# Moving the choice of batches 2 and 3 and their MLP two to three steps earlier in a fused retention and mixture-of-depths kernel

## The chip, the cores and the metric

The kernel runs on one core of one Trainium2 chip. The metric is the device time of one execution in microseconds (us). Engines are named as in the profile: PE is TensorE's matrix unit, PEld its weight load, DVE is VectorE, ACT is ScalarE, POOL is GpSimd, SP is SyncE, which here only starts transfers.

## The reference: what is computed

Eight batches, eight heads, 576 positions, head size 64. First a retention layer (attention without softmax, with a causal decay per head), then a mixture of depths: in each batch the 128 positions with the highest score get a two-layer MLP added, all others pass unchanged.

```python
scores = scale * np.matmul(q, k.transpose(0, 1, 3, 2))
ret = scores * Dmat                 # gamma_h ** (i - j) for j <= i, else 0
x = np.matmul(ret, v)               # bridged to (batch, position, 512)
s = np.einsum('bsd,d->bs', x, w_gate)
top_idx = np.argpartition(-s[b], 128)[:128]
ye = np.maximum(x[b, top_idx] @ w1, 0.0) @ w2          # 512 -> 1024 -> 512
out[b, top_idx] = x[b, top_idx] + sigmoid(s[b, top_idx])[:, None] * ye
```

## The kernel before

**Steps.** The program is one unrolled loop (line 660 on) over 36 steps and one more that drains; 9 steps make a group of two batches (`NC = 9`, `NG = 4`). Steps 0 to 8 are the "wide" group: a step is 128 positions, batches 0 and 1 one after the other. Steps 9 to 35 are three "pair" groups: a step is 64 positions of two batches side by side, so batches 2 and 3 are steps 9 to 17, batches 4 and 5 steps 18 to 26, batches 6 and 7 steps 27 to 35. The decays are carried as a running state `u_ps`, copied out to `st`, so that each step needs only its own block of scores and the state of the step before.

**A pair step on PE.** PE executes in the order in which the program is written. Step s issues, interleaved two by two: the scores `sc_ps` of step s with the value products `y_ps<-vs,am` of step s-1 (call this A); then a piece of MLP work; then the state sums `u_ps` of step s with the state products `y_ps<-st,raw` of step s-1 (call this B). DVE masks the scores (`am`, line 340), scales the result (`xs`, line 356) and forms the gate score of each position (`scored`, line 365). ACT scales the values (`vs`, line 224, eight instructions of one head each) in pair steps; in wide steps POOL does it in one instruction (line 219). POOL starts the stores of `xs`.

**Loads.** SP loads 256 KB pieces, four a step. From step 15 on a piece is started at a moment of PE's program (`tick`, line 153): one at the start of A, one behind A, one behind the MLP piece, one at the start of B. In the stretch that the change touches, step s starts the pieces of step s+2, and the last two of them are those that A needs.

**Choice.** When a group's nine steps are scored, PE spreads the scores along a row (`n_spread`, or `w_spread` for the wide group), ACT copies the row, DVE counts for each position how many are higher (`n_compare`, `n_late`, line 458: 576 columns wide for three of the nine blocks, 192 for six), turns ranks into one-hot rows (`n_chosen`, `hot`, nine instructions), PE turns these into indices (`n_fetch`, `idx_ps`), ACT casts them, and POOL gathers the 128 chosen rows of each batch from HBM (line 423, one indirect DMA a batch).

**MLP.** `mlp` and `ups` transpose the gathered rows on PE (`xg_ps`, line 504, in program order, at once) and put the rest into a queue of parts. `some(n)` takes n parts of the queue. A part of the upward product (`h_ps`) or of the downward one (`ye_ps`) has a size by how many batches it serves: for batches 0 and 1 each on its own (called half parts here, 4 matmuls of `ye_ps` or 16 narrow ones of `h_ps` in the profile), for batches 2 and 3 together (whole parts, 8 of `ye_ps` or 16 of `h_ps`), for batches 4 and 5 upward in half parts again (8 of `h_ps`). When a batch's last downward part is through, DVE forms `o` (line 530), which frees the one PSUM bank that `ye_ps` has, and POOL scatters the rows.

**The order.** A table written by hand, `at(step, place, function, ...)`, sets at which place of a step each function is issued; places 1, 2, 2.5 and 3 stand behind A, behind the MLP part, behind the wide results, and at the step's end. `n_parts` says how many parts each step takes between places 1 and 2.

**What the change and the prediction touch:** `scaled` (line 215), the table entries for the wide group's second spread (lines 597 to 599), for group 1's choice, gather and MLP (lines 623 to 632), `n_parts` (line 647), and the loop's calls of `scaled` (lines 669 and 692).

Of the kernel before, what the change touches and what calls it, by code (L numbers as in the profile page):

```python
# [13 lines left out]
OP = mybir.AluOpType  # L14
# [5 lines left out]
P = 128  # L20
# [27 lines left out]
def kernel(  # L48
# [17 lines left out]
    NS = qkvk.shape[0]  # L66
    DM, F = 512, 1024
    KD, FB = DM // P, F // P
    D = DM // H
    NG = len(KINDS)  # L70
    NC = NS // NG
# [3 lines left out]
    MIX = NC // 2  # L75
# [98 lines left out]
    decw = part_of("decw", 2 * NC * H).rearrange("p (s c h) -> p s c h", s=2, c=NC)  # L174
    dec = part_of("dec", 2 * NC * H).rearrange("p (s c h) -> p s c h", s=2, c=NC)
# [19 lines left out]
    def tables():  # L195
        nc.vector.tensor_scalar(aheadw[:, BEFOREW : BEFOREW + P], causw, TINY, -TINY,
                                op0=OP.mult, op1=OP.add)
        nc.vector.tensor_scalar(ahead[:, BEFORE : BEFORE + C], caus, TINY, -TINY,
                                op0=OP.mult, op1=OP.add)
        nc.vector.tensor_copy(out=place, in_=part_of("place", 2 * NC).rearrange(  # L200
            "p (a b) -> p a b", b=2))
        nc.vector.tensor_copy(out=placew, in_=part_of("placew", 2 * NC).rearrange(
            "p (a b) -> p a b", a=2))
# [9 lines left out]
    kind = lambda s: KINDS[s // NC]  # L213

    def scaled(s):
        k = s % NC
        vs[s] = work.tile([P, DM], F32, name="vs", bufs=4)
        if kind(s) == "wide":
            return nc.gpsimd.tensor_tensor(out=heads(vs[s]), in0=heads(raw[s][:, 2, :]),
                                           in1=decw[:, 0, k, :].unsqueeze(2).to_broadcast([P, H, D]),  # L220
                                           op=OP.mult)
        else:
            for h in range(H):
                nc.scalar.activation(out=vs[s][:, hd[h]], in_=raw[s][:, 2, hd[h]], func=AF.Copy,  # L224
                                     scale=dec[:, 0, k, h : h + 1])

    wide_heads = [(j, i, HJ * i + j) for j in range(HJ) for i in range(2)]
    jd = [slice(D * j, D * j + D) for j in range(HJ)]
# [2 lines left out]
    def w_scores(s):  # L231
        for i in range(2):
            sc_ps[s, i] = bank("sc_ps", "sc")
        first = None
        for j, i, h in wide_heads:
            ins = mm(sc_ps[s, i][:, jt[j]], raw[s][halves[i], 1, jt[j]],
                     raw[s][halves[i], 0, jt[j]], True, True)
            first = first or ins
        return first

    def w_sums(s):
        k = s % NC
        if k == NC - 1:
            return
        if k in (0, MIX):
            u_ps[s // NC, k >= MIX] = bank("u_ps", "u", 1)
        u = u_ps[s // NC, k >= MIX]
        rows = halves[1] if k == MIX else slice(0, P)
        for j, i, h in wide_heads:
            mm(u[halves[i], jd[j]], raw[s][rows, 3, hd[h]], vs[s][rows, hd[h]],  # L250
               k in (0, MIX) and j == 0, k in (MIX - 1, NC - 2))

    def w_masked(s):
        am[s] = work.tile([P, 2, 512], F32, name="am")
        mask = mixw if s % NC == MIX else causw
        v = lambda t: t.rearrange("p (j t) -> p j t", t=P)
        for i in range(2):
            nc.vector.tensor_tensor(out=v(am[s][:, i, :]), in0=v(sc_ps[s, i]),  # L258
                                    in1=mask.unsqueeze(1).to_broadcast([P, HJ, P]), op=OP.mult)

    def w_state(s):
        if s % NC < NC - 1:
            st[s] = work.tile([P, DM], F32, name="st")
            nc.scalar.copy(out=st[s][:, : HJ * D], in_=u_ps[s // NC, s % NC >= MIX][:, : HJ * D])
# [27 lines left out]
    def n_open(s):  # L292
        k = s % NC
        sc_ps[s] = bank("sc_ps", "sc")
        for h in range(H):
            for half in halves:
                yield lambda h=h, half=half: mm(sc_ps[s][half, hd[h]], raw[s][half, 1, hd[h]],
                                                raw[s][half, 0, hd[h]], True, True)
# [13 lines left out]
    def n_values(s):  # L312
        k = s % NC
        y_ps[s] = bank("y_ps", "y")
        for h in range(H):
            for i, half in enumerate(halves):
                yield lambda h=h, i=i, half=half: mm(
                    y_ps[s][halves[1 - i], hd[h]], am[s][half, 0, hd[h]], vs[s][half, hd[h]],
                    h == 0, k == 0)
# [10 lines left out]
    def in_turn(a, b, moments):  # L330
        for n in range(H):
            for f in (next(a, None), next(a, None), next(b, None), next(b, None)):
                if f:
                    f()
            if n in moments:
                tick(AHEAD if n == 0 else 2)

    def n_masked(s):
        am[s] = work.tile([P, 2, 512], F32, name="am")
        nc.vector.tensor_tensor(out=heads(am[s][:, 0, :]), in0=heads(sc_ps[s]),  # L340
                                in1=caus.unsqueeze(1).to_broadcast([P, H, C]), op=OP.mult)
# [26 lines left out]
    def stored(s):  # L368
        g, k = divmod(s, NC)
        if kind(s) == "pair":  # L370
            nc.gpsimd.dma_start(out=outs[2 * g][k], in_=xs[s])  # L371
        elif k == MIX:
            nc.gpsimd.dma_start(out=outs[2 * g][P * k :], in_=xs[s][:C])
            nc.gpsimd.dma_start(out=outs[2 * g + 1][:C], in_=xs[s][C:])
        else:
            t0 = P * k - (S if k > MIX else 0)
            nc.gpsimd.dma_start(out=outs[2 * g + (k > MIX)][t0 : t0 + P], in_=xs[s])
# [63 lines left out]
    EARLY = 2 * NC // 3  # L441
# [117 lines left out]
    def some(n):  # L559
        for _ in range(min(n, len(parts))):  # L560
            f, a = parts.popleft()
            f(*a)
# [4 lines left out]
    plan = {}  # L567

    def at(slot, where, f, *a):
        plan.setdefault((slot, where), []).append((f, a))  # L570

    def do(slot, where):
        for f, a in plan.get((slot, where), []):
            f(*a)
# [6 lines left out]
    T1, T3, T4, T5 = P * 3, S, P * (MIX + 3), 2 * S  # L581
# [12 lines left out]
    at(7, 2.5, w_fetch, 0, 0)  # L594
    at(9, 3, ups, 0)

    at(7, 2.5, w_spread, 0, MIX, MIX + 3)
    for c in range(MIX, MIX + 3):
        at(8, 1, w_compare, 0, 1, c, T3, T4, 0)
    at(9, 3, w_spread, 0, MIX + 3, NC)  # L600
    for c in range(MIX, MIX + 3):
        at(10, 1, w_compare, 0, 1, c, T4, T5, 1)
# [14 lines left out]
    for g in range(1, NG):  # L617
        s = NC * g + EARLY + 1
# [3 lines left out]
               n_compare, g, c, 0, EARLY)  # L622
    s = 2 * NC
    at(s + 1, 2, n_spread, 1, EARLY, NC)
    for c in range(EARLY, NC):
        at(s + 1, 3, n_late, 1, c)
    for c in range(EARLY):
        at(s + 2, (1, 3)[c // 3], n_late, 1, c)
    at(s + 3, 3, n_chosen, 1)
    at(s + 5, 1, n_fetch, 1)  # L630
    at(s + 7, 1, mlp, 2, 3)
    at(s + 7, 3, gates, 2, 3)
    s = 3 * NC
    at(s + 1, 2, n_spread, 2, EARLY, NC)
    for c in (*range(EARLY, NC), *range(EARLY)):
# [8 lines left out]
    at(s + 4, 3, gates, 4, 5)  # L644


    n_parts = {s: 1 if s < 34 else 2 for s in range(10, 37)}

    def ahead_of(s):
        if s <= LED:  # L650
            load(s, 1)
            load(s, 0)
        if s == 10:
            weight(0)
            weight(1)
# [6 lines left out]
    for s in range(NS + 1):  # L662
        pe["slot"] = s
        ahead_of(s + AHEAD)
        wide = s < NS and kind(s) == "wide"
        before = s > 0 and kind(s - 1) == "pair"
        if wide:
            first = w_scores(s)
            if kind(s + 1) == "wide":
                tc.add_manual_dep(scaled(s + 1).ins, first.ins.name, LANDED, reason="beside scores")  # L670
        if s in range(1, NC + 1) and s != NC - 1:
            stored(s - 1)
        if wide:
            w_sums(s)
            w_masked(s)
            w_state(s)
        else:
            in_turn(n_open(s) if s < NS else iter(()), n_values(s - 1) if before else iter(()),
                    (0,))
            if s < NS:  # L680
                n_masked(s)
        if s == MIX:
            tables()
        tick()
        do(s, 1)
        if s == NC - 1:
            stored(s - 1)
        scattered()
        some(n_parts.get(s, 0))
        tick()  # L690
        do(s, 2)
        if s + 1 < NS and kind(s + 1) == "pair":
            scaled(s + 1)
        if wide:
            w_results(s)
            do(s, 2.5)
            values(s)
        else:
            in_turn(n_sums(s) if s < NS else iter(()), n_states(s - 1) if before else iter(()),
                    (0, H // 2))  # L700
            if s < NS:
                n_state(s)
            if before:
                values(s - 1)
                for x in due.get(s, []):
                    scored(x)
                stored(s - 1)
        do(s, 3)
# [104 lines left out]
```

## Time and profile before

| what | value |
|---|---|
| three runs | 254.56, 255.22, 258.52 us; median 255.22 us |
| the profiled execution's own time | 253.84 us |
| its span in the profile | 252.1 us |
| PE busy | 230.0 us (91%) in 4595 matmuls |
| PEld, DVE, ACT, POOL busy | 177.0, 129.1, 104.8, 47.2 us |
| moved by DMA | 56.97 MB, of it 44.76 MB read from HBM and 11.53 MB written |

The page has a busy strip of 40 slices (6.3 us each) for each engine, the clock granted to PE, the chain of work that ended last, and groups of instructions. Views of the trace add the instructions in order of time ("timeline": start, duration, engine, line, operation, tiles, count, and in brackets the idle time before it and what ended it), the sums of busy time in chosen windows (busy us and instruction count for PE, PEld, DVE, ACT and POOL, then granted clock, DMA share, GB/s), the list of waits (total, times, longest), and the chain in order of time (start, duration, what).

### The profile page before, as it was taken

The numbers are of one execution on the slowest core, as the hardware profiler recorded it, in microseconds if no ns is written. First come the engines' busy times: TensorE is split into PE (matmuls) and PEld (weight loads), VectorE is DVE, ScalarE is ACT, GpSimd is POOL, SyncE is SP. The second block draws the span as 40 slices with busy tenths as digits, with TensorE's granted clock in tenths as the row PEclk, the third lists the DMA queues.
The fourth block names the chain that finished last, engine by engine and source line by source line (L and its number), as shares of the span: only waits on it lengthen the run. The fifth ranks groups of instructions, "written<-read, shape, count | busy, mean of one in ns | idle before, by whom it ended". The sixth has DMA issues, their size and how long they took to land.

```text
span 252.1 us, 10488 instructions
## 1 busy us (share of the span) xinstructions
PE 230.0 (91%) x4595; PEld 177.0 (70%) x4595; DVE 129.1 (51%) x342; ACT 104.8 (42%) x380; POOL 47.2 (19%) x67
## 2 busy tenths in 40 slices
PE   8997998894999979999779999999999998899991
PEld 6796886884998966656448888666688854588440
DVE  3455787582056539995435699536536492300011
ACT  2364365944455853854443455537251200211000
POOL 0624453002010100034002010403120004100011
PEclk9999999999599999999999999999999999999998
DMA  7989999999589869989957776788631102100011
GB/s 239 384 324 400 359 393 373 376 390 401 190 255 303 289 204 328 309 272 326 338 179 248 229 232 235 220 277 267 229 126 45 49 0 75 64 31 0 0 42 42
DMA packets 23085, 56.97 MB, mean 226 GB/s; under 512 B 2944, under 2 KB 3072, under 8 KB 23040
## 3 DMA queue, kind: packets, MB, share of 16 engines
q1 hardware_dynamic: 18864, 42.67, 49.5%
q0 software_dynamic: 4176, 13.63, 14.3%
q8 instruction: 36, 0.59, 1.0%
q14 instruction: 9, 0.07, 0.1%
HBM read 44.76 MB, written 11.53 MB: 223 GB/s over the span
## 4 chain that ended last, share of the span: by engine, by line
PE 72%; DMA 13%; issue 8%; ACT 3%; DVE 2%; POOLq 0%; SPq 0%; DVEq 0%; ACTq 0%
PE h_ps L157 24%; PE ye_ps L157 16%; DMA raw<-in_qkvk 11%; PE y_ps L157 11%; PE u_ps L157 8%; PE sc_ps L157 8%; ACT xs L353 1%; PE row_ps L157 1%; PE xg_ps L504 1%; DMA out<-o,idx 1%; DVE am L258 1%; ACT vs L224 1%; ACT xg L506 1%; DVE o L530 1%; PE idx_ps L157 1%
## 5 line engine op out<-in xcount | busy, mean ns | idle before, releaser
L157 PE MATMUL h_ps<-xg,w_sb 128*128 128x256 f32 (+1 forms) x320 | 62.6, 351 | 3.3 <-issue 1.9
L157 PE MATMUL ye_ps<-w_sb,hT 128*128 128x512 f32 x128 | 58.6, 602 | 0.6 <-DVE o L530 0.6
L157 PEld LDWEIGHTS h_ps<-xg,w_sb 128*128 128x128 f32 x320 | 52.3, 197 | 9.5 <-issue 2.1
L224 ACT ACTIVATE vs<-raw,table 128x64 f32<-128x64 f32 x216 | 54.3, 341 | 0.0
L157 PE MATMUL y_ps<-vs,am 64*64 64x64 f32 (+1 forms) x1152 | 41.9, 222 | 4.1 <-issue 3.5
L356 DVE TENSOR_TENSOR xs<-y_ps,table 128x512 f32<-128x512 f32 x27 | 18.6, 690 | 48.5 <-PE y_ps L157 48.4
L157 PE MATMUL sc_ps<-raw 64*64 64x64 f32 (+1 forms) x1008 | 42.1, 231 | 1.4 <-DMA raw<-in_qkvk 1.4
L157 PEld LDWEIGHTS y_ps<-vs,am 64*64 64x64 f32 (+1 forms) x1152 | 37.3, 136 | 5.3 <-issue 4.1
L157 PEld LDWEIGHTS ye_ps<-w_sb,hT 128*128 128x128 f32 x128 | 23.3, 190 | 24.9 <-issue 23.4
L157 PE MATMUL y_ps<-st,raw 64*64 64x64 f32 (+1 forms) x896 | 39.6, 232 | 1.1 <-ACT xs L353 0.7
L157 PEld LDWEIGHTS u_ps<-vs,raw 64*64 64x64 f32 (+1 forms) x896 | 30.1, 138 | 14.2 <-issue 9.1
L157 PEld LDWEIGHTS sc_ps<-raw 64*64 64x64 f32 (+1 forms) x1008 | 37.5, 145 | 3.3 <-issue 1.3
L371 POOL DMA_DIRECT2D out<-xs x27 | 14.9, 552 | 124.3 <-DVE xs L356 124.3
L157 PE MATMUL u_ps<-vs,raw 64*64 64x64 f32 (+1 forms) x896 | 35.3, 226 | 2.8 <-issue 2.4
L157 PEld LDWEIGHTS y_ps<-st,raw 64*64 64x64 f32 (+1 forms) x896 | 34.1, 144 | 3.5 <-issue 1.6
L518 ACT ACTIVATE hT<-h_ps 128x256 f32<-128x256 f32 (+1 forms) x24 | 10.9, 454 | 56.4 <-PE h_ps L157 56.4
L530 DVE SCALAR_TENSOR_TENSOR o<-ye_ps,gate,xr 128x512 f32<-128x512 f32 x8 | 6.0, 750 | 43.9 <-PE ye_ps L157 23.4
L458 DVE SCALAR_TENSOR_TENSOR scr<-row,sc,ahead 128x384 f32<-128x384 f32 (+2 forms) x45 | 26.0, 578 | 2.7 <-ACT row L451 1.5
L365 DVE SCALAR_TENSOR_TENSOR scr<-xs,wg 128x512 f32<-128x512 f32 x36 | 25.6, 712 | 1.0
L346 ACT COPY st<-u_ps 128x512 f32<-128x512 f32 x24 | 13.8, 575 | 17.0 <-PE y_ps L157 17.0
L340 DVE TENSOR_TENSOR am<-sc_ps,table 128x512 f32<-128x512 f32 x27 | 18.6, 687 | 3.7 <-PE sc_ps L157 1.9
L258 DVE TENSOR_TENSOR am<-sc_ps,table 128x512 f32<-128x512 f32 x18 | 11.6, 686 | 16.8 <-PE sc_ps L157 16.7
(51 smaller groups left out, 129.5 us busy)
## 6 DMA issues: line engine op xcount, KB each, us to landing
raw<-in_qkvk SPq DMA_DIRECT2D x84, 256.0 KB, 4.5
raw<-in_qkvk SPq DMA_DIRECT2D x30, 512.0 KB, 6.2
out<-xs POOLq DMA_DIRECT2D x35, 256.0 KB, 5.1
w_sb<-in_w SPq DMA_DIRECT2D x12, 256.0 KB, 4.2
w_sb<-in_w SPq DMA_DIRECT2D x2, 512.0 KB, 6.5
table<-in_consts SPq DMA_DIRECT2D x1, 314.0 KB, 6.0
wg<-in_w_gate SPq DMA_DIRECT2D x1, 256.0 KB, 4.7
out<-xs POOLq DMA_DIRECT2D x2, 128.0 KB, 6.2
```

Source lines behind the costliest of these rows:

```text
L157: pe["last"] = nc.tensor.matmul(out, w, x, start=start, stop=stop, skip_group_check=True)
L224: nc.scalar.activation(out=vs[s][:, hd[h]], in_=raw[s][:, 2, hd[h]], func=AF.Copy, scale=dec[:, 0, k, h : h + 1])
L258: nc.vector.tensor_tensor(out=v(am[s][:, i, :]), in0=v(sc_ps[s, i]), in1=mask.unsqueeze(1).to_broadcast([P, HJ, P]), op=OP.mult)
L340: nc.vector.tensor_tensor(out=heads(am[s][:, 0, :]), in0=heads(sc_ps[s]), in1=caus.unsqueeze(1).to_broadcast([P, H, C]), op=OP.mult)
L346: nc.scalar.copy(out=st[s], in_=u_ps[s // NC])
L353: nc.scalar.activation(out=xs[s][:, hd[h]], in_=y_ps[s, h // HJ][:, jd[h % HJ]], func=AF.Copy, scale=decw[:, 1, k, h : h + 1])
L356: nc.vector.tensor_tensor(out=heads(xs[s]), in0=heads(y_ps[s]), in1=dec[:, 1, k, :].unsqueeze(2).to_broadcast([P, H, D]), op=OP.mult)
L365: nc.vector.scalar_tensor_tensor(scr, xs[s], 1.0, wg, op0=OP.mult, op1=OP.mult, accum_out=sc[g][:, k : k + 1])
L371: nc.gpsimd.dma_start(out=outs[2 * g][k], in_=xs[s])
L458: nc.vector.scalar_tensor_tensor(scr[:, : C * (c1 - c0)], row[g][:, C * c0 : C * c1], sc[g][:, c : c + 1], ahead[:, at + C * c0 : at + C * ...
L518: nc.scalar.activation(out=hT[group][:, f0 : f0 + n, :w], in_=t, func=AF.Relu)
L530: nc.vector.scalar_tensor_tensor(o[:cap], ye[b][:cap], gate[b][:cap], xr[b][:cap], op0=OP.mult, op1=OP.add)
```

## The change: what it does

- **Values of step 9.** `scaled(9)` is one POOL instruction with the pair decays, in place of eight on ACT. It is issued in step 8 behind the first score matmul.
- **A spread in step 8.** The wide group's second spread (columns 4 to 6, three PE transposes and one ACT copy) moves from step 7, place 2.5, to step 8, place 2; its three compares move from place 1 to place 3 of step 8.
- **Choice of batches 2 and 3.** Six compares at the end of step 19 (three before), the last three in step 20 at place 1, the one-hot rows at the end of step 20 (21 before), indices and gathers in step 21 (23 before).
- **MLP of batches 2 and 3.** The transposes stand at the end of step 22 (before: in step 25), so the eight whole parts run in steps 23 to 30 (before: 26 to 33).
- **Parts.** Steps 19, 20 and 21 take a second half part at their end, so that the queue of batches 0 and 1 is empty after step 22 (before: after step 25). Step 31 takes none; steps 32 to 36 take one half part each of batches 4 and 5 (before: steps 34 to 36 two each). Eleven parts are left for the tail, ten before.

```diff
     def scaled(s):
         k = s % NC
+        by = (decw if kind(s) == "wide" else dec)[:, 0, k, :]
         vs[s] = work.tile([P, DM], F32, name="vs", bufs=4)
-        if kind(s) == "wide":
+        if s <= NC:
             return nc.gpsimd.tensor_tensor(out=heads(vs[s]), in0=heads(raw[s][:, 2, :]),
-                                           in1=decw[:, 0, k, :].unsqueeze(2).to_broadcast([P, H, D]),
-                                           op=OP.mult)
+                                           in1=by.unsqueeze(2).to_broadcast([P, H, D]), op=OP.mult)
...
-    at(7, 2.5, w_spread, 0, MIX, MIX + 3)
+    at(8, 2, w_spread, 0, MIX, MIX + 3)
     for c in range(MIX, MIX + 3):
-        at(8, 1, w_compare, 0, 1, c, T3, T4, 0)
+        at(8, 3, w_compare, 0, 1, c, T3, T4, 0)
...
     s = 2 * NC
     at(s + 1, 2, n_spread, 1, EARLY, NC)
-    for c in range(EARLY, NC):
-        at(s + 1, 3, n_late, 1, c)
-    for c in range(EARLY):
-        at(s + 2, (1, 3)[c // 3], n_late, 1, c)
-    at(s + 3, 3, n_chosen, 1)
-    at(s + 5, 1, n_fetch, 1)
-    at(s + 7, 1, mlp, 2, 3)
-    at(s + 7, 3, gates, 2, 3)
+    for c in (*range(EARLY, NC), *range(EARLY)):
+        at(s + 1 + (c in (3, 4, 5)), 1 if c in (3, 4, 5) else 3, n_late, 1, c)
+    at(s + 2, 3, n_chosen, 1)
+    at(s + 3, 2, n_fetch, 1)
+    at(s + 4, 3, mlp, 2, 3)
+    at(s + 5, 3, gates, 2, 3)
...
-    n_parts = {s: 1 if s < 34 else 2 for s in range(10, 37)}
+    n_parts = {s: int(s != 31) for s in range(10, 37)}
+    for s in (19, 20, 21):
+        plan.setdefault((s, 3), []).insert(0, (some, (1,)))
...
-            if kind(s + 1) == "wide":
+            if s + 1 <= NC:
                 tc.add_manual_dep(scaled(s + 1).ins, first.ins.name, LANDED, reason="beside scores")
...
-        if s + 1 < NS and kind(s + 1) == "pair":
+        if NC < s + 1 < NS:
             scaled(s + 1)
```

**ACT in steps 7 and 8.** Here `idx` is the cast of batch 0's indices, the first `xs` are the eight results of step 7, `row` is the copy of the spread, `vs` the values of step 9 and the next `xs` the results of step 8:

```order
 L264 COPY st<-u_ps 128x256
 L438 CAST idx<-idx_ps 128x1
+L353 ACTIVATE xs<-y_ps,table 128x64 x8
 L390 COPY row<-row_ps 128x384
-L353 ACTIVATE xs<-y_ps,table 128x64 x8
-L224 ACTIVATE vs<-raw,table 128x64 x8
 L353 ACTIVATE xs<-y_ps,table 128x64 x8
 L224 ACTIVATE vs<-raw,table 128x64 x8
```

The results of step 7 now stand ahead of the row copy, and eight `vs` instructions are gone.

**DVE in steps 20 and 21.** `am`, `xs` and `scr,sc` are a step's masked scores, result and gate score; line 458 are the compares of group 1, `o` is batch 0's MLP result, `hot` the one-hot rows. Before:

```order
L458 SCALAR_TENSOR_TENSOR scr_1936,rank<-row,sc,ahead 128x192
L340 TENSOR_TENSOR am<-sc_ps,table 128x512
L530 SCALAR_TENSOR_TENSOR o<-ye_ps,gate,xr 128x512
L356 TENSOR_TENSOR xs<-y_ps,table 128x512
L365 SCALAR_TENSOR_TENSOR scr,sc<-xs,wg 128x512
L467 TENSOR_TENSOR rank<-rank 128x6
L471 TENSOR_SCALAR hot<-table,rank 128x128 x9
```

After the change, from the last compare of step 19 on:

```order
L458 SCALAR_TENSOR_TENSOR scr_1834,rank<-row,sc,ahead 128x192
L340 TENSOR_TENSOR am<-sc_ps,table 128x512
L458 SCALAR_TENSOR_TENSOR scr_1875,rank<-row,sc,ahead 128x192
L458 SCALAR_TENSOR_TENSOR scr_1877,rank<-row,sc,ahead 128x192
L458 SCALAR_TENSOR_TENSOR scr_1879,rank<-row,sc,ahead 128x192
L530 SCALAR_TENSOR_TENSOR o<-ye_ps,gate,xr 128x512
L356 TENSOR_TENSOR xs<-y_ps,table 128x512
L365 SCALAR_TENSOR_TENSOR scr,sc<-xs,wg 128x512
L467 TENSOR_TENSOR rank<-rank 128x6
L471 TENSOR_SCALAR hot<-table,rank 128x128 x9
```

Before, `o` stood in step 21 behind that step's `am`; now it stands in step 20, behind that step's `am` and the last three compares, and the one-hot rows follow in step 20.

**PE in step 31.** Before, and then after the change; `ye_ps` is a whole part of batch 3, `xg_ps` are the transposes of the rows of batches 4 and 5 that have just been gathered:

```order
L157 MATMUL sc_ps<-raw 64x64 x2
L157 MATMUL y_ps<-vs,am 64x64 x2
L157 MATMUL ye_ps<-w_sb,hT 128x512 x4
L504 MATMUL xg_ps<-table,xr 128x128 x8
L157 MATMUL u_ps<-vs,raw 64x64 x2
```

```order
L157 MATMUL sc_ps<-raw 64x64 x2
L157 MATMUL y_ps<-vs,am 64x64 x2
L504 MATMUL xg_ps<-table,xr 128x128 x8
L157 MATMUL u_ps<-vs,raw 64x64 x2
L157 MATMUL y_ps<-st,raw 64x64 x2
```

The part that stood between A and the transposes is gone from step 31.

More of the change, by code (lines that the diff above doesn't have):

```diff
@@ L224, in scaled @@
                 nc.scalar.activation(out=vs[s][:, hd[h]], in_=raw[s][:, 2, hd[h]], func=AF.Copy,
-                                     scale=dec[:, 0, k, h : h + 1])
+                                     scale=by[:, h : h + 1])
     wide_heads = [(j, i, HJ * i + j) for j in range(HJ) for i in range(2)]
```

## The prediction

> **What bounds the kernel now.** I read the page's strips and its chain first, then PE's waits in two stretches, then windows between those waits, then the timeline at the three places of the change.
>
> ```profile
> PEclk9999999999599999999999999999999999999998
> PE 72%; DMA 13%; issue 8%; ACT 3%; DVE 2%; POOLq 0%; SPq 0%; DVEq 0%; ACTq 0%
> q8 instruction: 36, 0.59, 1.0%
> ```
>
> PE carries the chain, and 8% of the span is "issue", time in which it waited for nothing the profile names. The instruction queue moved 0.59 MB in 36 packets, 16 KB each. PE's 4595 matmuls and as many weight loads make 9190 instructions, 255 a packet.
>
> PE's waits from 96 to 130 us, which are steps 19 to 25:
>
> ```profile
> PE u_ps L157 <- issue: 2.4, 4, 1.3
> PE xg_ps L504 <- issue: 1.8, 1, 1.8
> PE sc_ps L157 <- DMA raw<-in_qkvk: 0.3, 1, 0.3
> ```
>
> These sum to 4.5 us. The windows run from the end of one issue wait to the end of a later one; the first two columns are PE busy with its count, then PEld:
>
> ```profile
> 105.07:109.66 4.59, 4.15 (x127) 2.71 (x127) 4.41 (x17) 2.50 (x9) 0.54 (x1) 1.00 0.90 278
> 109.66:118.41 8.75, 8.41 (x254) 5.53 (x254) 6.31 (x19) 5.21 (x20) 3.26 (x5) 1.00 0.94 296
> 118.41:124.09 5.68, 4.34 (x128) 2.83 (x128) 1.99 (x4) 2.50 (x9) 1.51 (x2) 1.00 0.95 334
> 124.09:128.87 4.78, 2.68 (x127) 2.37 (x128) 2.08 (x4) 0.59 (x1) 0.58 (x1) 1.00 0.90 316
> ```
>
> The waits fall every 128 matmuls (127 to 128, and twice that). So PE's program comes in blocks of 256 instructions, and the next block is not there sooner than 4.4 to 5.7 us after the last. A step without row spreads is about one block. If its work takes less than that, PE stands still for the rest, whatever else is ready: **steps with a half part are paced by the refill, steps with a whole part are not**. From 130 to 200 us, where whole parts run, the list of PE's waits is empty.
>
> [...]
>
> **The change, part by part.** The sum is made against the profiled execution's 253.84 us; the median of the runs, 255.22 us, lies 1.4 us above it.
>
> *Steps 7 to 9.* The rows are of ACT and PE:
>
> ```profile
> 39.87 0.16 ACT L438 CAST idx<-idx_ps 128x1 int32<-128x1 f32 x1 [2.06 <-PE idx_ps L157]
> 40.68 0.32 PE L388 MATMUL row_ps<-table,sc 128*128 128x128 f32 x1 [0.48 <-DVE scr L365]
> 41.47 1.75 ACT L353 ACTIVATE xs<-y_ps,table 128x64 f32<-128x64 f32 x8
> 43.05 2.06 ACT L224 ACTIVATE vs<-raw,table 128x64 f32<-128x64 f32 x8
> 43.27 1.10 PE L157 MATMUL y_ps<-st,raw 64*128 64x64 f32 x14 [0.39 <-ACT xs L353]
> 49.35 0.63 ACT L506 COPY xg<-xg_ps 128x512 f32<-128x512 f32 x1
> 50.03 0.38 PE L157 MATMUL h_ps<-xg,w_sb 128*128 128x128 f32 x1 [0.67 <-ACT xg L506]
> ```
>
> ACT holds back `xs` of step 7 until the row copy, which waits for a PE transpose, which waits for a DVE score; PE's step 8 then waits for that `xs`. With the spread in step 8, `xs` starts behind the cast, at 40.03 instead of 41.47: **1.4 us** earlier, and ACT, then the `h_ps` at 50.03, follow. Bounds: 0.7 (only the wait before 43.27 and half of the 0.67) to 1.9 (0.48 + 0.36 + 0.39 + 0.67, every wait in these rows and the one before 42.45). I take 1.4, the row with the direct cause. The 2.06 us of `vs` taken off ACT I cost at nothing: they ran from 43.05 beside PE's products of step 8, which take from 43.27 to 45.38. POOL's own `vs` take 1.08 us on average, between its gather (to 41.5) and the store behind it; step 9's sums need it about 45. Without that cover it would cost 1.1.
>
> *Steps 19 to 26.* From the half part of step 19 to the part of step 26, in the chain in order of time; the last two rows are whole parts in quiet steps:
>
> ```profile
> 97.75 1.91 PE ye_ps L157 x4
> 99.67 0.49 PE row_ps L157 x12
> 115.71 0.31 PE idx_ps L157 x9
> 132.50 0.63 PE row_ps L157 x22
> 134.12 3.65 PE h_ps L157 x16
> 167.33 0.87 PE xg_ps L504 x8
> 170.23 3.63 PE ye_ps L157 x8
> 175.88 3.63 PE ye_ps L157 x8
> ```
>
> It takes 134.12 - 97.75 = 36.4 us. A and B together take 175.88 - 170.23 - 3.63 = 2.0. Work: seven half parts 13.4, seven times A and B 14.1, the spreads, indices and transposes 2.3; 29.8 in all. So 6.6 us are standing, 4.5 of them named above, the rest in small delays of the same steps. After the change steps 19 to 21 take 2.0 + 1.9 + 1.9 = 5.8 us, step 22 4.8 with its transposes, steps 23 to 25 5.7: nearly all longer than the refill, and the loads get the same time. The 6.6 go. What comes in their place is on DVE:
>
> ```profile
> 101.78 0.81 DVE L458 SCALAR_TENSOR_TENSOR scr<-row,sc,ahead 128x576 f32<-128x576 f32 x1
> 104.24 0.69 DVE L340 TENSOR_TENSOR am<-sc_ps,table 128x512 f32<-128x512 f32 x1
> 104.85 0.41 DVE L458 SCALAR_TENSOR_TENSOR scr<-row,sc,ahead 128x192 f32<-128x192 f32 x1
> 109.31 0.74 DVE L530 SCALAR_TENSOR_TENSOR o<-ye_ps,gate,xr 128x512 f32<-128x512 f32 x1
> ```
>
> In step 20 the second part is batch 1's first, and `ye_ps` has one bank: it waits for batch 0's `o`. DVE starts the compares at 101.78 as before; three wide ones to 104.24, three narrow at 0.45 to 105.6, `am` to 106.2, three narrow to 107.6, `o` to 108.3. PE is there at 97.75 + 1.91 + 0.49 + 1.0 + 1.91 + 1.0 + 1.91 + 1.0 = 107.0. **PE waits 1.4.** Queued behind `o` are `xs` and the one-hot rows, ready near 111.9; PE wants them near 113. Then the gather of step 21 has until the transposes of step 22; with a landing of 5.0 us (below) it is just in time, 0.3 taken, and 0.4 for one refill about steps 22 to 23, which hold only 4.8. Saved: 6.6 - 2.1 = **4.5 us**. Bounds: 6.6, and 2.3 if the gather takes the 7.7 us of its old place.
>
> *Steps 31 to 36.* The three whole parts moved up leave step 31 without one, and half parts in steps 32 to 36. The rows are POOL's second gather, the landing times of that pair and of the pair in step 23, the starts and landing times of step 32's loads, and the part that now covers them:
>
> ```profile
> 161.03 0.99 POOL L423 DMA_INDIRECT xr<-out,idx  x1 [0.30 <-issue]
> DMA to landing us min/median/max: 3.4/4.2/5.0
> DMA to landing us min/median/max: 7.2/7.5/7.7
> 161.70 1.61 SPq L153 DMA_DIRECT2D raw<-in_qkvk  x3
> DMA to landing us min/median/max: 6.0/6.1/6.2
> 163.70 3.63 PE ye_ps L157 x8
> ```
>
> Without the part PE reaches the transposes at 163.70. The first batch's rows are there; the second's land at 161.03 + 5.0 = 166.0, so behind 0.4 of work PE waits 1.9. Then 0.4 and B end at 167.5, but step 32's last needed piece, the second of the three started from 161.70, lands about 168.5: 0.9 more. Steps 32 to 36 hold 2.0 + 1.9 = 3.9 us of work each and meet the refill pace of 4.4 again: 0.5 each while loads run, less behind step 33, together 2.0. **Given back: 4.8 us.** Bounds: 1.0 (landing in 3.4, refills almost hidden on the quieter queue) to 7.6 (landing in 7.7, waits 4.6, and 3.0). The tail's extra half part is the same PE work, moved.
>
> Sum: -1.4 - 4.5 + 4.8 = -1.1. 253.84 becomes 252.7, and a median of runs 255.22 - 1.1 = **254.1 us**: no difference that a measurement of this kernel can tell, which I put at 2%, 5.1 us.
>
> **Rivals.** *The end is not starved:* step 31's gather lands in 3.4 us and refills are quick because the loads run out; 1.0 is given back. -1.4 - 4.5 + 1.0 = -4.9, 250.3 us. For it: DMA share is low behind step 33. Against: the 5.0 us landing, which is in a trace with as many loads.
>
> *The gather stops PE's clock, slower than before:* in step 31 PE has nothing but the gather. One long stop stands in the trace:
>
> ```profile
> PE y_ps L157 <- issue: 3.3, 1, 3.3
> 63.03 3.71 PE h_ps L157 x16
> 69.71 1.98 PE h_ps L157 x16
> 74.15 1.98 PE h_ps L157 x16
> ```
>
> Behind 3.3 us of standing, the strip shows the clock at half, and the step from 63.03 took 6.7 us where the next took 4.4: 2.2 lost. If the gather lands in 7.7 us, PE stands 4.6 in one piece; with the clock that is 6.8, and the load is covered. -1.4 - 4.5 + 6.8 + 2.0 = +2.9, 258.1 us. It decides from a landing of some 6.4 us on. Against: 5.0 measured here. [...]
>
> *The issue waits don't follow the pace:* then the 4.2 named ones stay wherever the parts are, the middle saves 6.6 - 4.2 - 2.1 = 0.3, the end gives back the 2.8 of step 31. -1.4 - 0.3 + 2.8 = +1.1, 256.3 us. [...] Against: the spacing of 128 and the empty list behind 130 us.
>
> **How the numbers follow.** Chances: forecast 0.45, end not starved 0.27, clock stopped 0.12, issue waits fixed 0.16. Faster by over 2%, below 250.1, is nearly half of the second case and 0.07 of the forecast's: 0.20. Slower, above 260.3, needs the clock stopped and the bad bounds of the other terms: 0.07. Within 2%: 0.73. The range reaches from just below the second case to just above the third: 249.5 to 258.8 us.
>
> **What would show it.** Right: no issue wait in steps 19 to 21; one `ye_ps` wait on `o` of 1 to 2 us in step 20; `h_ps` of step 10 about 48.6; an `xg_ps` or `sc_ps` wait near step 31 of 2 to 3 us; issue waits of `u_ps` or `sc_ps` in steps 32 to 36. Wrong: an empty list of PE's waits behind step 31, or issue waits in steps 19 to 21 as large as before, or a second dip in the clock strip.

## The result, and the profile after

| | before | after |
|---|---|---|
| median of 20 runs each, taken together | 255.04 us | 258.15 us |
| lowest and highest | 251.83 and 259.30 | 255.15 and 262.03 |
| the profiled execution, and its span | 253.84, 252.1 | 258.94, 257.2 |

The ratio after to before is 1.0121, 95% interval 1.0086 to 1.0157: the change costs about 3.1 us where a gain of 1.1 was forecast. A second set of the same kernel (e9) gave 1.0198, 1.0129 to 1.0268. Executions more than 1.5% above the fastest of their kernel (seven of e10's twelve) are left out of every ratio, and the profiles of e6 and e10, which are such executions, are not read.

The strip of the clock and the chain by engine, from the page of the changed kernel (40 slices of 6.4 us):

```profile
PEclk9799999999799999999999999989999999999998
PE 74%; DVE 8%; DMA 8%; issue 6%; ACT 2%; POOLq 0%; POOL 0%; SPq 0%; DVEq 0%
```

Two things are new against the strip of before: a dip in the second slice (the clock is at half from 9.04 to 12.45 us), which comes and goes between executions of one kernel (e7 has none there, e11, the same kernel, has one), and one in the 27th (at half from 166.05 to 169.46). "issue" went from 8 to 6%, and DVE is now on the chain with 8%.

**The middle came out as forecast.** PE's waits from 96 to 130 us of the changed kernel:

```profile
PE ye_ps L157 <- DVE o L530: 1.2, 1, 1.2
```

That is the whole list: the 4.2 us of issue waits are gone, and the one wait on `o` in step 20 has come. One window from the half part of step 19 to the MLP part of step 26, after and then before (columns: window and length, then PE, PEld, DVE, ACT, POOL busy):

```profile
97.80:140.51 42.71, 41.52 (x997) 29.98 (x993) 25.71 (x70) 20.28 (x73) 8.32 (x12) 1.00 0.77 249
```

```profile
97.68:134.05 36.37, 31.81 (x949) 21.68 (x945) 24.15 (x66) 19.47 (x69) 7.38 (x11) 1.00 0.87 290
```

The window now also holds the three whole parts that came from behind it, 3 x 3.63 = 10.9 us. 36.37 + 10.9 - 42.71 = 4.6 us saved.

**The end lost twice what was forecast.** The last matmul starts at 246.35 us before and at 251.44 after, so 5.1 later, while step 26's part starts at 134.05 and 140.51, so 6.5 later, and 10.9 of work is gone: 5.1 - 6.5 + 10.9 = 9.5 us lost, against 4.8. PE's waits from 162 to 212 us of the changed kernel:

```profile
PE u_ps L157 <- issue: 2.0, 3, 1.0
PE y_ps L157 <- issue: 1.5, 1, 1.5
PE u_ps L157 <- ACT vs L224: 1.2, 1, 1.2
PE idx_ps L157 <- DVE hot L471: 0.4, 1, 0.4
PE sc_ps L157 <- DMA raw<-in_qkvk: 0.2, 1, 0.2
```

The gather's wait that was forecast here (1.9) is not in it. Three things are: refills in steps 31 to 36 (3.5), a wait on ACT (1.2), and a small one of 0.4 in step 30 that is followed by a larger loss. "Refill" stands here and below for PE's waits on issue, read as waits for the next block of instructions; these four end at 175.56, 180.79, 185.11 and 194.10 us, with 128, 127 and 255 matmuls between them. The small one begins on DVE. The timeline of DVE, steps 28 to 30, after:

```profile
155.57 0.75 DVE L530 SCALAR_TENSOR_TENSOR o<-ye_ps,gate,xr 128x512 f32<-128x512 f32 x1 [0.61 <-PE ye_ps L157]
156.24 0.68 DVE L356 TENSOR_TENSOR xs<-y_ps,table 128x512 f32<-128x512 f32 x1
156.95 0.69 DVE L365 SCALAR_TENSOR_TENSOR scr<-xs,wg 128x512 f32<-128x512 f32 x1
...
157.57 0.81 DVE L458 SCALAR_TENSOR_TENSOR scr<-row,sc,ahead 128x576 f32<-128x576 f32 x1
...
163.60 0.68 DVE L471 TENSOR_SCALAR hot<-table,rank 128x128 f16<-128x128 f32 x3
```

and before:

```profile
148.43 0.68 DVE L356 TENSOR_TENSOR xs<-y_ps,table 128x512 f32<-128x512 f32 x1
149.15 0.69 DVE L365 SCALAR_TENSOR_TENSOR scr<-xs,wg 128x512 f32<-128x512 f32 x1
...
150.00 0.82 DVE L458 SCALAR_TENSOR_TENSOR scr<-row,sc,ahead 128x576 f32<-128x576 f32 x1 [0.16 <-ACT row L451]
...
156.04 1.85 DVE L471 TENSOR_SCALAR hot<-table,rank 128x128 f16<-128x128 f32 x9
```

Since the MLP of batches 2 and 3 runs three steps earlier, batch 2's `o` now ends in step 28, and stands on DVE ahead of `xs`, the scores and the nine compares of the next choice; DVE first waits 0.61 for its `ye_ps`, then spends 0.75 on it. PE spreads the scores at 149.0 before and 155.5 after, so the first one-hot row comes 7.0 us behind the spread before and 8.1 after. PE's side of it, the index product of step 30 and the clock around it (windows; the column of ones is the granted clock):

```profile
163.94 1.74 PE L157 MATMUL idx_ps<-place,hot 128*128 128x2 f16 x9 [0.39 <-DVE hot L471]
```

```profile
163.94:166.05 2.11, 1.96 (x10) 1.08 (x11) 2.11 (x9) 0.33 (x3) 0.00 (x0) 1.00 0.88 303
166.05:169.46 3.41, 3.41 (x5) 1.33 (x4) 1.30 (x3) 1.80 (x8) 2.44 (x3) 0.50 0.37 117
```

That `o` is what makes the one-hot rows late is read from this order and its two times; no run moves `o` alone. Nine small products now follow the one-hot rows at DVE's pace, 1.74 us in place of 1.05, and then the clock is at half for 3.41 us. In the chain in order of time the whole part behind them, after and then before:

```profile
165.69 5.24 PE ye_ps L157 x8
```

```profile
158.13 3.54 PE ye_ps L157 x8
```

From the part of step 26 to the end of step 30's part the changed kernel loses 2.8 us (0.4 wait, 0.7 for the indices, 1.7 for the part); steps 31 to 36 and the tail lose the other 6.7 (4.9 in the waits listed, the rest in small delays beside them).

The profiled executions differ by 5.1 us and the medians by 3.1. Batch 0's indices come at 41.2 us after and 39.5 before, in code that is the same in both; over the profiles of this study that moment lies between 38.2 and 42.9, with and without the change. From there to step 19's half part the changed kernel takes 56.6 us in place of 58.2, so that this part starts at the same time in both (97.80 and 97.68), and the 5.1 us are those of the middle and the end.

### The profile page after: what moved, and what is told of

Same layout as the page of the kernel before. It is cut to its first block, busy times and chain, and to the rows that moved or that the text cites. A ratio compares the mean times of both kernels' runs of the same rounds, so it can differ in the third digit from the quotient of the medians.

```text
span 257.2 us, 10478 instructions
## 1 busy us (share of the span) xinstructions
PE 232.3 (90%) x4595; PEld 177.4 (69%) x4595; DVE 128.8 (50%) x342; ACT 102.7 (40%) x372; POOL 48.1 (19%) x68
## 4 chain that ended last, share of the span: by engine, by line
PE 74%; DVE 8%; DMA 8%; issue 6%; ACT 2%; POOLq 0%; POOL 0%; SPq 0%; DVEq 0%
PE h_ps L157 24%; PE ye_ps L157 17%; PE y_ps L157 13%; PE sc_ps L157 9%; PE u_ps L157 8%; DVE scr L458 4%; DMA raw<-in_qkvk 4%; DMA xr<-out,idx 3%; DVE o L530 1%; DMA out<-o,idx 1%; PE xg_ps L504 1%; PE idx_ps L157 1%; PE row_ps L157 1%; DVE scr L365 1%; DVE xs L356 1%
## 5 line engine op out<-in xcount | busy, mean ns | idle before, releaser
L157 PE MATMUL ye_ps<-w_sb,hT 128*128 128x512 f32 x128 | 60.4, 617 | 1.8 <-DVE o L530 1.8
L157 PEld LDWEIGHTS h_ps<-xg,w_sb 128*128 128x128 f32 x320 | 51.4, 194 | 7.2 <-ACT xg L506 1.0
L224 ACT ACTIVATE vs<-raw,table 128x64 f32<-128x64 f32 x208 | 52.1, 340 | 0.0
L157 PE MATMUL y_ps<-vs,am 64*64 64x64 f32 (+1 forms) x1152 | 42.8, 224 | 6.4 <-issue 5.9
L157 PEld LDWEIGHTS y_ps<-vs,am 64*64 64x64 f32 (+1 forms) x1152 | 38.1, 137 | 7.7 <-issue 6.6
L157 PE MATMUL y_ps<-st,raw 64*64 64x64 f32 (+1 forms) x896 | 39.0, 231 | 1.6 <-issue 1.5
L518 ACT ACTIVATE hT<-h_ps 128x256 f32<-128x256 f32 (+1 forms) x24 | 10.9, 454 | 57.6 <-PE h_ps L157 57.5
```

The source lines that it names most:

```text
L157: pe["last"] = nc.tensor.matmul(out, w, x, start=start, stop=stop, skip_group_check=True)
L518: nc.scalar.activation(out=hT[group][:, f0 : f0 + n, :w], in_=t, func=AF.Relu)
```

## The experiments

**The theory** after the result: (1) the refill pace left steps 19 to 25 and now holds back steps 31 to 36, in which the blocks are as short as they were in the middle; (2) the choice of the next group is late by batch 2's `o`, and the clock falls in step 30; (3) the gain of the front is taken back by refills in steps 11 to 16. **The rivals**: the loss is one of the front edits; the doubled half parts cost by themselves; the loss is a mishap of single executions.

**e1: the front edits alone** (on the kernel before).

```diff
-    at(7, 2.5, w_spread, 0, MIX, MIX + 3)
+    at(8, 2, w_spread, 0, MIX, MIX + 3)
-        at(8, 1, w_compare, 0, 1, c, T3, T4, 0)
+        at(8, 3, w_compare, 0, 1, c, T3, T4, 0)
-        if kind(s) == "wide":
+        if s <= NC:
```

> The kernel before with the edits of steps 7 to 9 alone (values of step 9 on GpSimd, the spread and its compares in step 8). Main theory: ScalarE reaches step 7's results 1.4 us sooner and PE's h_ps of step 10 follows; nothing later takes it back: ratio 0.993 to 0.997, time between the indices of batch 0 and the second B of step 10 shorter by 1.2 to 1.9 us. Rival (the front is the loss): ratio 1.005 or more. Rival (taken back by the instruction refill behind step 10): ratio 0.999 to 1.002, and a longer stop in step 11.

Measured: 0.9988 (0.9934 to 1.0042), so -0.3 us, somewhere between -1.7 and +1.1: it can be told neither from no change nor from the -1.4 forecast. PE's waits from 36 to 62.6 us, e1 and then before:

```profile
PE y_ps L157 <- issue: 4.2, 1, 4.2
PE xg_ps L504 <- DMA xr<-out,idx: 1.0, 1, 1.0
PE h_ps L157 <- issue: 0.3, 1, 0.3
```

```profile
PE y_ps L157 <- issue: 3.3, 1, 3.3
PE y_ps L157 <- ACT xs L353: 0.7, 2, 0.4
PE h_ps L157 <- ACT xg L506: 0.7, 1, 0.7
PE h_ps L157 <- issue: 0.6, 1, 0.6
PE row_ps L388 <- DVE scr L365: 0.5, 1, 0.5
```

The waits on ACT and DVE that the forecast counted (0.7, 0.7, 0.5) are gone. In their place PE waits 1.0 for the gathered rows, which nothing hides any more, and 0.9 longer on issue (4.2 in place of 3.3): read as a refill, PE came earlier to blocks that did not. The gain is there all the same: from batch 0's indices to the end of step 10's part e1 takes 11.9 us in place of 13.3, and to step 19's half part 57.1 in place of 58.2. It goes in steps 19 to 25. The window from step 19's half part to step 26's part, and PE's waits from 95 to 134 us, in e1:

```profile
95.52:133.87 38.35, 32.93 (x949) 22.88 (x946) 24.25 (x66) 19.52 (x69) 7.32 (x11) 0.96 0.84 275
```

```profile
PE u_ps L157 <- issue: 4.0, 4, 2.1
PE y_ps L157 <- issue: 1.4, 1, 1.4
```

That is 2.0 us more than the 36.37 before, with 5.4 of issue waits in place of 4.2, and the clock at half from 125.63 to 129.04. So part (3) of the theory has its place wrong in this profile: the gain is taken back for the most part in steps 19 to 25, by refills and the clock, and not in steps 11 to 16.

**e2: the change without the front edits.**

```diff
-    at(8, 2, w_spread, 0, MIX, MIX + 3)
+    at(7, 2.5, w_spread, 0, MIX, MIX + 3)
-        at(8, 3, w_compare, 0, 1, c, T3, T4, 0)
+        at(8, 1, w_compare, 0, 1, c, T3, T4, 0)
-        if s <= NC:
+        if kind(s) == "wide":
```

> The changed kernel with the edits of steps 7 to 9 undone, so the choice, the parts and the MLP of batches 2 and 3 alone. Main theory (the loss stands behind step 29 and the front helps): 1.012 and the 1.4 us of the front on top, ratio 1.015 to 1.019. Rival (the front is the loss): ratio 0.995 to 1.003.

Measured: 1.0148 (1.0090 to 1.0206). The loss is in the rest of the change, not in the front. Its waits from 140 to 212 us:

```profile
PE u_ps L157 <- issue: 3.1, 2, 2.4
PE idx_ps L157 <- DVE hot L471: 0.4, 1, 0.4
...
```

The 0.4 of the index product is here again, and the clock is at half from 167.44 to 170.85. Behind the refill wait of 2.4 in step 32 it is at half once more, from 184.51.

**e3: the end filled** (the change, with 28 products of zeros; at the rate of a whole part, 0.46 us each, that is 12.8 us of work, and it is in no output).

```diff
+    at(31, 1, filler, 8)
+    for s in range(32, 37):
+        at(s, 1, filler, 4)
```

> The changed kernel with extra matmuls on a table of zeros that nothing reads: as many as a whole part in step 31, as a half part in each of steps 32 to 36; 28 matmuls of 256 columns in the program, 12.8 us of PE work by the rate of 3.65 us for eight. Main theory (these steps are shorter than the refill of the instructions, PE stands 5 to 6.8 us in them): the extra work fills the standing, so the time rises by 6 to 8.5 us over the changed kernel, not by 12.8; no issue wait of over 0.5 us is left in steps 31 to 36. Rival (PE's work sets these steps, the loss is elsewhere): 12 to 13.5 us.

Measured: 1.0373 (1.0293 to 1.0453), 2.5% or 6.4 us over the change's 1.0121; against its second set, 1.0198, it would be 4.5. So 6.4 to 8.3 of the 12.8 us went into time in which PE stood (e3's own interval is 2 us either way). All that is left of its waits from 140 to 205 us:

```profile
PE idx_ps L157 <- DVE hot L471: 0.4, 1, 0.4
```

**e5: the middle filled** (the kernel before, with 28 such products in steps 19 to 25).

```diff
+    for s in range(19, 26):
+        at(s, 1, filler, 4)
```

> The kernel before with extra matmuls on a table of zeros that nothing reads, as many as a half part in each of steps 19 to 25: 28 matmuls of 256 columns, 12.8 us of PE work. The mirror of the filled end. Main theory (6.6 us of standing for the instruction refill in these steps): time rises by 6 to 8 us, no issue wait of over 0.5 us is left from 97 us to the transposes of step 25. Rival (PE's work sets these steps): 12 to 13.5 us.

Measured: 1.0209 (1.0153 to 1.0265), 5.4 us for 12.8 of work. So 7.4 us stood there in the kernel before; 6.6 was worked out. No wait of PE is left between 97 and 131 us. e3 and e5 are the same test at the two places: 12.8 us of added work cost 4.5 to 6.4 us there and 5.4 here, half its time or less, in steps that a wait holds back, and such steps are what the change moved from one place to the other.

**e6: only the doubled half parts** (on the kernel before).

```diff
+    for s in (19, 20, 21):
+        plan.setdefault((s, 3), []).insert(0, (some, (1,)))
```

> The kernel before with the second half part in each of steps 19 to 21 alone; the choice and the MLP of batches 2 and 3 stay, so steps 23 and 24 have no part. Main theory (a step costs the longer of its work and the refill, so moving parts between paced steps moves the standing only): issue waits leave steps 19 to 21 and appear in steps 22 to 24, each of the two empty steps standing over 2 us: ratio 0.996 to 1.008. Rival (the doubled steps are the gain by themselves): ratio 0.98 to 0.99.

Measured: 1.0126 (1.0050 to 1.0203), worse than expected. Doubling is no gain by itself: steps 23 and 24 are left without a part, and the MLP of batches 2 and 3 starts one step earlier, in step 25. Where exactly it loses stays open.

**e8: work ahead of the indices** (the change, with three products of zeros in step 30 so that PE doesn't stand there).

```diff
+    plan[30, 1].insert(0, (filler, (3,)))
```

> The changed kernel with three extra matmuls on zeros (1.4 us) between A and the indices in step 30, where PE waited 0.4 us for the first one-hot rows, was fed them one by one, and the clock was at half for 3.4 us. Main theory (VectorE, 1.1 us late because batch 2's result now stands ahead of the step's scores, starves PE there and the clock falls): the extra matmuls stand in time that was waited, the clock stays, 1 to 2 us less than the changed kernel, ratio 1.004 to 1.009. Rival (the drop is chance, it comes in some executions alone): ratio 1.011 to 1.017.

Measured: 1.0201 (1.0154 to 1.0248); the gain expected did not come. Its waits from 140 to 212 us:

```profile
PE xg_ps L504 <- DMA xr<-out,idx: 2.4, 1, 2.4
PE h_ps L157 <- issue: 2.2, 1, 2.2
...
```

The wait on the one-hot rows is gone and the clock stays up in step 30 (no `ye_ps` matmul from 155 to 186 us takes over 0.70 us, where the changed kernel's take up to 1.06), but PE then reaches step 31's transposes sooner and waits 2.4 for the gather, and the clock is at half right behind, from 176.07. The clock's fall in step 30 was hiding the gather; taking one away shows the other, and e9 below shows the same without the products of zeros. The ratio also holds the stops in step 21 (below; 1.2 us of issue waits in this profile's list, as in e9's) that the changed kernel's first profile does not have; e9, with the same stops, is level with it at 1.0198.

**e4: the parts spread evenly** (the change, with the MLP of batches 2 and 3 in 16 half parts, one a step and two in eight chosen steps).

```diff
+    def second_half():
+        mlp(2, 3, size=1)
-    at(s + 4, 3, mlp, 2, 3)
+    at(s + 4, 3, second_half)
-    n_parts = {s: int(s != 31) for s in range(10, 37)}
+    n_parts = {s: 1 for s in range(10, 37)}
+    n_parts |= {s: 2 for s in (24, 26, 29, 30, 32, 34, 35, 36)}
```

> The changed kernel with the MLP of batches 2 and 3 in sixteen half parts spread over steps 23 to 33 (two in steps 24, 26, 29, 30, 32, one in the others), and two half parts of batches 4 and 5 in each of steps 34 to 36 as before, so that no step from 23 on is without a part. Main theory (the loss is the starved end): steps with one half part stand 0.4 us each, six of them, in place of some 9.6 us from step 26 on; 255.0 - 1.4 - 4.5 + 2.5 = 251.6 us, ratio 0.98 to 0.993. Rival (half parts cost more than whole ones, or the middle itself is the loss): ratio 1.0 to 1.01.

Measured: 0.9886 (0.9816 to 0.9957). Its waits from 140 to 212 us:

```profile
PE xg_ps L504 <- DMA xr<-out,idx: 1.9, 1, 1.9
PE ye_ps L157 <- DVE o L530: 0.6, 1, 0.6
PE sc_ps L157 <- DMA raw<-in_qkvk: 0.6, 1, 0.6
PE y_ps L157 <- issue: 0.4, 1, 0.4
```

Batch 2's `o` falls in step 30 now, behind the choice; there is no wait on the one-hot rows, no dip of the clock between 63 us and the tail (granted clock over the span 0.988, before 0.982), and the refills are down to 0.4.

**e7: the same, doubled in other steps**, to give the gather of step 30 cover as well.

```diff
-    n_parts |= {s: 2 for s in (24, 26, 29, 30, 32, 34, 35, 36)}
+    n_parts |= {s: 2 for s in (24, 26, 27, 30, 31, 34, 35, 36)}
```

> The kernel with even parts, with two half parts in steps 24, 26, 27, 30, 31 and one in 28, 29, 32, 33: the gather of batches 4 and 5 has one half part more behind it, and step 29 one less. Main theory: the 1.9 us that the transposes of step 31 waited for the gather go, and one paced step comes: 0.5 to 1.5 us below the even parts, ratio to before 0.978 to 0.99. Rival (the place of the single steps doesn't matter): equal to the even parts within 0.5 us, the waits only elsewhere.

Measured: 1.0147 (1.0077 to 1.0217), a miss. Its waits from 140 to 212 us, and the clock behind them:

```profile
PE sc_ps L157 <- DMA raw<-in_qkvk: 1.5, 1, 1.5
PE idx_ps L157 <- DVE hot L471: 0.6, 1, 0.6
PE y_ps L157 <- issue: 0.5, 1, 0.5
```

```profile
165.57:168.98 3.41, 3.39 (x7) 1.67 (x8) 2.20 (x6) 2.13 (x10) 1.55 (x2) 0.50 0.37 141
```

The gather's wait is gone as expected, but with a single part in step 29 PE comes to the loads and the one-hot rows too soon, and pays with the clock (at half for 3.41 us). The stops in step 21 are in this profile too (1.3 us of issue waits), and add to the time.

**e9, e10, e11: the change, e4 and e7 once more, side by side on one chip**, in five rounds.

> The changed kernel itself, taken once more on one chip with the two kernels behind it, so that the three can be laid beside each other. Main theory (its loss is a thing of its order: batch 2's o ahead of the scores in step 28, the stop and the clock in step 30, the refills of steps 32 to 36): 1.009 to 1.016 of the kernel before, and the clock at half near 166 us again. Rival (the loss is a mishap of single executions): within 0.995 to 1.005.

> The version with two half parts in steps 24, 26, 29, 30, 32, 34, 35 and 36 once more, on the same chip as the changed kernel. Main theory (it spreads the work so that step 30 keeps its part and steps 32 to 36 hold more than a refill): 0.982 to 0.996 of the kernel before and 2 to 3% below the changed kernel; no wait of the index product on the one-hot rows in step 30. Rival (the first measurement was a lucky chip, as the next version's 1.015 on another chip suggests): 1.000 to 1.015.

> The version with the doubled parts in steps 24, 26, 27, 30, 31, 34, 35 and 36 once more, on the same chip. Main theory (step 29 with a single part lets PE reach the index product of step 30 before the one-hot rows and its clock falls, some 2.5 us, and the rest of its first loss was that one execution's): 0.995 to 1.008. Rival (the order itself loses in steps 20 to 22 too): 1.012 to 1.02 with the small waits of step 21 there again.

Measured: 1.0198 (1.0129 to 1.0268), 1.0016 (0.9957 to 1.0074) and 1.0240 (1.0165 to 1.0314). The order of the three holds, and all three are about 1% dearer than in their first sets. e4 is 1.0016 / 1.0198 = 0.982 of the change; by the medians of all their executions, 259.11 and 260.83 us, it is 0.7% under it, so how much it gains is not settled. Against the kernel before it is better in one set and level in the other, so it is not shown to beat it. e9 rules out the mishap, though it lies above the range expected of it (1.009 to 1.016); e10 is inside its rival's range and not its main one; e11 is above both its ranges and nearer its rival's, whose stops in step 21 it has. The clock at half near 166 us, expected of e9, did not come. Its waits from 162 to 212 us show what came instead:

```profile
PE xg_ps L504 <- DMA xr<-out,idx: 2.6, 1, 2.6
PE sc_ps L157 <- DMA raw<-in_qkvk: 1.1, 1, 1.1
PE y_ps L157 <- issue: 0.9, 1, 0.9
PE idx_ps L157 <- DVE hot L471: 0.4, 1, 0.4
```

```profile
167.27 1.75 PE L157 MATMUL idx_ps<-place,hot 128*128 128x2 f16 x9 [0.40 <-DVE hot L471]
168.88 3.68 PE L157 MATMUL ye_ps<-w_sb,hT 128*128 128x512 f32 x8
```

```profile
171.94 5.89 DMA xr<-out,idx
```

```profile
177.41:180.82 3.41, 2.86 (x72) 2.56 (x76) 0.00 (x0) 1.74 (x7) 0.00 (x0) 0.50 0.95 350
```

The same 0.40 in step 30, and the part behind it at full clock, 3.68. So PE is at step 31's transposes early, the second gather takes 5.9 us to land (the chain in order of time), PE waits 2.6, a load costs 1.1, refills 0.9: the forecast's gather, load and refill (1.9, 0.9, 2.0) in one trace, the load in step 34 and not in step 32. And behind the 2.6 the clock is at half from 177.41. The loss behind step 26 is 8.5 us here.

**Why e9 and e10 are dearer than the first sets.** In e7, e8, e9 and e11, on two chips, step 21's products crawl. The timeline of PE in e9:

```profile
116.27 0.27 PE L157 MATMUL y_ps<-st,raw 64*64 64x64 f32 x2 [0.40 <-issue]
...
117.01 0.28 PE L157 MATMUL u_ps<-vs,raw 64*64 64x64 f32 x2 [0.41 <-issue]
...
117.75 0.31 PE L157 MATMUL y_ps<-st,raw 64*64 64x64 f32 x2 [0.38 <-issue]
```

Three stops, 0.74 us apart, with a handful of instructions between them; B takes 3.6 us in place of 1.2. Of the 4.6 us saved in the middle this leaves:

```profile
98.28:143.84 45.56, 43.00 (x998) 30.83 (x994) 25.84 (x70) 20.40 (x73) 8.34 (x12) 1.00 0.72 238
```

36.37 + 10.9 - 45.56 = 1.7. The changed kernel's first profile, e2, e3 and e4 have no such stops (e2 to e4 on a third chip). For e9, 2.0 us dearer by its ratio than the first set, the stops are enough. That e10 is 3.3 dearer than e4 for the same reason is likely, and not shown. For e11 they explain nothing, since e7 has them as well. In these profiles it goes with the chip, at the same place of one order, but each chip was also used at one time only; what makes it is open.

## Why the prediction was wrong, point by point

- **What bounds the kernel: right.** Steps with a half part are held back by something other than PE's work: e5 put 12.8 us of work into them for 5.4, and no wait of PE was left between 97 and 131 us. That this is the refill is read from the spacing of the issue waits, 128 matmuls or twice that also in steps 31 to 36 after the change (5.23, 4.32 and 8.99 us); no run takes it apart from other causes.
- **Steps 7 to 9 (-1.4): the direct cause was right; whether its size lasts to the end is open.** The waits named are gone. `h_ps` of step 10 starts at 50.63, not at 48.6, because that execution was 1.7 late before the first edit acts: measured from batch 0's indices it is 9.4 behind in place of 10.6, so 1.2 earlier, with a gather wait of 1.0 ahead of it that the step had not. At step 19's half part 1.6 is gained in the changed kernel's profile and 1.1 in e1's, but over eight profiles with the front edits this distance lies anywhere from 54.8 to 58.9 us, and in before and e2, which lack them, it is 58.2 and 58.7. In e1 it is gone by step 26. The forecast let a gain in the front pass through stretches that its own first part calls paced by the refill.
- **Steps 19 to 26 (-4.5): right**, 4.6 in the changed kernel's profile, with a wait on `o` of 1.2 where 1.4 was worked out. On a chip where step 21 crawls, 1.7.
- **Steps 31 to 36 (+4.8): the term that was mis-sized.** The loss behind step 26 is 9.5 us in one profile and 8.5 in the other. In the second the three items are there at 2.6, 1.1 and 0.9, 4.6 together; the term lacked the clock behind the gather's wait (1.5), all of step 30 (1.1 here, 2.8 in the first), and 1.3 of small delays. In the first the gather's wait of 1.9 is not there; the refills are 3.5 in place of 2.0, and the wait of 1.2 on ACT was not thought of. The step that failed is the sentence that takes the term from the transposes of step 31 on. Step 30 was taken as standing work, though its choice waits for DVE, and a whole MLP had been moved ahead of it on DVE. The forecast asked what `o` does to DVE in step 20, where it found 1.4 us, and did not ask it in step 28, where batch 2's `o` is new.
- **Rivals.** "The clock stopped" gave 258.1 us, and the median is 258.15. That the number agrees is luck: the changed kernel's first profile, from that set, has no gather wait at all. Its mechanism is that of e9, with the point from which it decides put too high: it was priced at 4.6 us of standing and was to decide from a landing of 6.4; in e9 the clock fell behind a wait of 2.6 and a landing of 5.9. In the first profile the clock falls one step earlier, behind another wait, and the gather is then hidden. "Not starved" and "the waits don't follow the pace" are out by e3 and e5.
- **The sign to watch for** was among those listed: a second dip in the clock strip.

With the end at 9.5 the forecast's own sum is -1.4 - 4.5 + 9.5 = +3.6, against 3.1 measured. So it is the end's term that turned the sign, whatever the front's share is.

## What to carry to other kernels

Work that is moved ahead takes its own tail with it: for each moved piece, list what its last instructions (here one `o` on DVE) now stand ahead of, in every later step and not just in the one under study. Where a stretch is bound by a pace, a gain ahead of it can be taken back there (e1: 1.1 us ahead at step 19's half part, and 2.0 us longer from there to step 26's part), and emptying a later stretch to fill this one moves the loss; try spreading the same work evenly first (e4 is under the change in both sets). And two waits that hide each other are priced as a pair: e8 removed one of 0.4 us and got the other, 2.4 us.

## What the runs showed of the hardware

- **A wait of 0.4 us was followed by a fall of the clock in two executions, and not in two others.** The falls of these executions lie on a grid. In the changed kernel's profile the clock is at half from 9.04, 63.65 and 166.05 us, for 3.41 us each time, and the falls are 54.61 and 102.40 us apart, 16 and 30 times 3.413 (together 157.01, 46 times); in the kernel before it is at half from 61.97 to 68.80, twice 3.413; in e9 it falls at 10.16, 61.36 and 177.41, 15 and 34 times 3.413 apart. The 0.4 us wait and nine index products (1.7 us, 0.18 each) in step 30 were followed by a fall in the changed kernel's first profile and in e2, and not in e3 and e9. In the first the pair (163.55 to 165.68) lies between two lines of the grid, 162.64 and 166.05, and in e2 (164.57 to 166.72) between the lines at 164.03 and 167.44. In e9 the wait ends at 167.27, just behind a line at 167.17, and ahead of the next line the products share the time with dense work (PE busy for all of 168.90 to 172.50); in e3 the pair (165.70 to 167.85) is cut by a line at 167.20, 23 times 3.413 behind the fall at 88.69. That the place on the grid decides is the author's reading of these four executions; no run tests it.
- **PE stopped at a steady beat for nothing the profile names:** in e9 0.4 us every 0.74 us (above), 2.4 us in one step. The same waits, 1.2 to 1.3 us in each list from 96 to 130 us, stand in the four profiles e7, e8, e9 and e11 of the changed order's step 21 on two chips, and in none of three (e2, e3, e4) on a third.
